# A gate half formed from a copy of the even part in 32 of 288 units of a Fourier and feed-forward kernel

## The chip, the cores and the metric

The kernel runs on one core of a Trainium2 chip. The time is that of one execution on the device, in microseconds (us). The engines are named as in the profile: PE is TensorE (matmuls), PEld its weight loads, DVE is VectorE, ACT is ScalarE, POOL is GpSimd and SP is SyncE, whose queue issues the DMA transfers. PSUM holds the results of matmuls; SBUF holds everything else that is on the core.

## The reference

`x` has shape 8 x 3008 x 256. The reference takes the real part of its two-dimensional Fourier transform (along 3008 and along 256), sees the result as 24064 tokens of 256 values, and sends it through a feed-forward block with a gate:

```python
def _attn_ref(x):
    X = np.fft.fft(x, axis=1)
    X = np.fft.fft(X, axis=2)
    return X.real.astype(np.float32)

def _moe_ref(x, w_gate, w_val, w_out):
    g = x @ w_gate                                   # 256 -> 1536
    gelu = 0.5 * g * (1.0 + erf(g / sqrt(2)))
    val = x @ w_val                                  # 256 -> 1536
    return (gelu * val @ w_out).astype(np.float32)   # 1536 -> 256
```

## The kernel before

**Two rows of tokens from one set of columns.** The transform of a real input is symmetric: row m and row 3008 - m have the same even part and an odd part of opposite sign. For each of the 8 batches the kernel therefore holds only 1505 columns in `Y`, `Y[:, 0]` the even part and `Y[:, 1]` the odd part (channels on the partitions, tokens along the free dimension). The channel transform is folded into the weights once at the start: `WE` multiplies the even part, `WOP` the odd part, each with a gate half (index 0) and a value half (index 1). A token of the plus rows has gate and value WE·even + WOP·odd, one of the minus rows WE·even - WOP·odd. `WOM` is -2 times `WOP`, with one row treated apart (`col_m`): added on to a bank of PSUM that holds the plus rows, it turns them into the minus rows. That one row's share is `nq` (one value a token) times `WN` (one value a channel of the hidden layer), where it has to be added by other engines; `gen_wn` (L411) computes `WN` with 24 one-column matmuls during batch 0.

**Units and pairs.** The first layer is cut into 288 units: 8 batches, in each 3 chunks of columns (`CH`: 481 columns from 1024 on, then 0 to 511, then 512 to 1023), in each chunk 12 blocks of 128 hidden channels. A unit is known by u, its place in its batch by i = u % 36; i below 12 is the chunk of 481 columns. Two units that follow one another, an even and an odd one, are a pair, which shares tiles of two halves: `pv` (PSUM, values), `glp` and `glm` (gelu of the gate for plus and minus rows), `ev` and `dv`.

**The order of the work.** The order on each engine is the order of the program text. In iteration u of the main loop (from L864 on) TensorE gets:

1. `val_even(u)` (L602): one pass of WE into `ps_v`. VectorE makes `ev` = nq·WN + even part of the value.
2. `gate_minus(u-1)` (L613): one pass of WOM on to the bank `ps_g` of unit u-1, which ScalarE has already read once; ScalarE makes `glm`.
3. `val_odd(u-1)` (L634): one pass of WOP on to `ps_v`. If u-1 closes a pair, VectorE makes the plus rows of `h` = glp·pv for both units in one instruction, and `dv` = 2·ev - pv in another, which is the value of the minus rows.
4. `gate_plus(u)` (L618): passes of WE and WOP into a fresh `ps_g`; ScalarE makes `glp`.
5. `minus(u-1)` (L654): if u-1 closes a pair, GpSimd makes the minus rows of `h` = glm·dv for both units.
6. Work for later batches: the fold of x (`fold_x`, L210, on GpSimd: two tensor_tensor and a cast, in some odd units), the first stage of the transform (`a_step`, L462: two matmuls and an evacuation by ScalarE, i from 0 to 11), the second stage (`b_steps`, 47-column matmuls put between the passes, in units from 18 on) with evacuations `Y` by ScalarE.
7. `second(...)` (L877): 8 matmuls of the second layer from a list of steps, `ps_o` <- `Wo_sb`, `h`, evacuated by ScalarE as `osb` and stored by SP's queue. In the later units of a chunk 6 steps are taken where the list is short.

The first chunk of batch 0 goes another way (`kind` 0), without ev and dv.

**What waits for what.** PSUM has two buffers of `ps_g`, so the WE pass of unit u+2's gate needs the readers of unit u's bank to be done; two double buffers of `ps_v` (one a pair); one `ps_o` and one `ps_d`. The folded input `xf` has two buffers, one for even and one for odd batches. `h` has two buffers of 12 x 1024 columns. At u % 12 == 0 the loop makes the second-layer list of the chunk that has just ended; where that is the chunk from column 0 (i = 24) it also copies, on GpSimd, column 960 of the older tile of h into column 1023 of the newer one.

Of the kernel before, what the change touches and what calls it, by code (L numbers as in the profile page):

```python
# [9 lines left out]
FP32 = mybir.dt.float32  # L10
BF16 = mybir.dt.bfloat16
# [16 lines left out]
def _sub(base: bass.AP, free_pattern, free_offset, part_start=0, part_num=None):  # L28
    p_step, p_count = base.ap[0]
    if part_num is None:  # L30
        part_num = p_count - part_start
    pat = [[p_step, part_num]] + [list(x) for x in free_pattern]
    off = base.offset + part_start * p_step + free_offset
    return ap_replace(base, ap=pat, offset=off)
# [3 lines left out]
def kernel(  # L38
# [28 lines left out]
    HJ = 24  # L67
# [24 lines left out]
    WOP = const_pool.tile([128, 2, F], BF16)  # L92
    WOM = const_pool.tile([128, 2, F], BF16)
    Wo_sb = const_pool.tile([128, NFC, C], BF16)
    WNb = const_pool.tile([128, NFC], BF16)
    WN = const_pool.tile([128, NFC], FP32)
    NQs = [const_pool.tile([128, YW], BF16, name=f"nq{i}") for i in range(2)]
    HXF = NFC - NCH * 2
    hx = const_pool.tile([128, HXF, 128], BF16)
    xf_bufs = [const_pool.tile([128, HJ, 2, 128], BF16, name=f"xf{i}") for i in range(2)]  # L100

    Ap = const_pool.tile([128, NG, C], BF16)

# [33 lines left out]
    def glp_tile():  # L137
        return work.tile([128, 2, 512], BF16, tag="glp", bufs=2, name="glp")

    def glm_tile():  # L140
        return work.tile([128, 2, 512], BF16, tag="glm", bufs=3, name="glm")

    def ev_tile():
        return work.tile([128, 2, 512], FP32, tag="ev", bufs=2, name="ev")

    def dv_tile():
        return work.tile([128, 2, 512], FP32, tag="dv", bufs=2, name="dv")

    def osb_tile():
        return work.tile([128, 2, C], FP32, tag="osb", bufs=2, name="osb")  # L150
# [8 lines left out]
    def ps_v():  # L159
        return psum.tile([128, 2, 512], FP32, tag="v", bufs=2, name="ps_v")  # L160
# [48 lines left out]

    def fold_x(b, i, eng, a0=0, an=8, other=None):  # L210
        xt = xins[i]
        xf = xf_bufs[b % 2]
        o0 = (8 * i + a0) * C
        lo = _sub(xt, [[C, an], [1, 127]], a0 * C + 1)
        hi = _sub(xt, [[C, an], [-1, 127]], a0 * C + 255)
        ea = _sub(xf, [[C, an], [1, 127]], o0 + 1)
        od = _sub(xf, [[C, an], [1, 127]], o0 + 129)
        eng.tensor_tensor(ea, lo, hi, op=ALU.add)
        eng.tensor_tensor(od, lo, hi, op=ALU.subtract)
        (other or eng).tensor_copy(  # L220
            _sub(xf, [[C, an], [128, 2]], o0), _sub(xt, [[C, an], [128, 2]], a0 * C))
# [188 lines left out]

    def gen_wn():  # L411
        ps = ps_d()
        for fc in range(NFC):
            for t in range(NCH):
                pe.matmul(
                    ps[:, fc : fc + 1], _sub(wb[(fc // 4 * 512, 1)], [[1, 128]], t * 512 + fc % 4 * 128),
                    CW[:, t, 1, 0:1], start=(t == 0), stop=(t == NCH - 1))
        vec.tensor_copy(WNb[:, :], ps[:, :NFC])
        vec.tensor_copy(WN[:, :], WNb[:, :])

    def gen_tf():
        for i, t in enumerate((TP, TQ, T0P)):
# [38 lines left out]

    def a_step(b, k):  # L462

        xf = xf_bufs[b % 2]
        if "S1" not in st[b]:
            st[b]["S1"] = S1_tile()
        S1 = st[b]["S1"]
        if b == 0:
            ps = (ps_g, ps_vh, ps_o if k % 8 < 4 else ps_d, ps_vh)[k % 4]()
        else:  # L470
            ps = ps_o() if b == 1 and k % 2 and 1 < k < 10 else ps_d()
        for i in range(2):
            jj = 2 * k + i
            on_half(ps, pe.matmul(
                ps[:, i * C : (i + 1) * C], G[:, jj, :], _sub(xf, [[1, C]], jj * C),
                start=True, stop=True))
        dst = _sub(S1, [[1, 2 * C]], 2 * k * C)
        if b == 0 and k % 2 == 0 and k >= 8 or b == 1 and k in (0, 3, 5, 7, 9):
            return on_half(ps, vec.tensor_copy(dst, ps))
        return on_half(ps, act.activation(dst, ps, AF.Copy))  # L480
# [85 lines left out]


    units = []
    for b in range(B):
        for ci in range(len(CH)):  # L570
            for fc in range(NFC):
                units.append((b, ci, fc))
    hs, banks, duos = {}, {}, {}

    def kind(u):
        b, ci, fc = units[u]
# [2 lines left out]
    def open_unit(u):  # L579
        b, ci, fc = units[u]  # L580
        if fc == 0:
            hs[(b, ci)] = h_tile()
        c0, n = CH[ci]
        if u % 2 == 0:
            duos[u // 2] = dict(pv=ps_v(), glp=glp_tile(), glm=glm_tile(), log=[])
            if kind(u):
                duos[u // 2]["ev"] = ev_tile()
        banks[u] = dict(
            d=duos[u // 2], k=u % 2, pv=duos[u // 2]["pv"][:, u % 2, :],
            glp=duos[u // 2]["glp"][:, u % 2, :], glm=duos[u // 2]["glm"][:, u % 2, :],  # L590
            b=b, fc=fc, c0=c0, n=n, nm=n - n % 32, kd=kind(u), fs=slice(fc * 128, (fc + 1) * 128),
            h=hs[(b, ci)], Y=Ys[b], nq=NQs[b % 2], po=0 if n == 512 else 480,
            mo=512 if n == 512 else 0)

    def layer1(r, ps, W, i, eo, n, start):
        m = pe.matmul(
            ps[:, :n], W[:, i, r["fs"]], r["Y"][:, eo, r["c0"] : r["c0"] + n],
            start=start, stop=True, skip_group_check=not start)
        if i:
            apart(r["d"]["log"], r["k"], m)  # L600

    def val_even(u):  # L602
        r = banks[u]
        layer1(r, r["pv"], WE, 1, 0, r["n"], True)
        if r["kd"]:
            nm, fc = r["nm"], r["fc"]
            apart(r["d"]["log"], r["k"], vec.scalar_tensor_tensor(
                r["d"]["ev"][:, r["k"], :nm], r["nq"][:, r["c0"] : r["c0"] + nm],
                WN[:, fc : fc + 1], r["pv"][:, :nm], op0=ALU.mult, op1=ALU.add))
        else:  # L610
            layer1(r, r["pv"], WOP, 1, 1, r["n"], False)

    def gate_minus(u):  # L613
        r = banks[u]
        layer1(r, r["pg"], WOM, 0, 1, r["nm"], False)
        act.activation(r["glm"][:, : r["nm"]], r["pg"][:, : r["nm"]], AF.Gelu)

    def gate_plus(u, fill):  # L618
        r = banks[u]
        n = r["n"]  # L620
        r["pg"] = ps_g()
        layer1(r, r["pg"], WE, 0, 0, n, True)
        fill()
        layer1(r, r["pg"], WOP, 0, 1, n, False)
        fill()
        act.activation(r["glp"][:, :n], r["pg"][:, :n], AF.Gelu)
# [27 lines left out]
    def minus(u):  # L654
        r = banks.pop(u)
        if r["kd"] and r["k"]:
            nm, d = r["nm"], r["d"]
            hm = _sub(r["h"], [[1024, 2], [-1, nm]], (r["fc"] - 1) * 1024 + r["mo"] + nm - 1)
            pool.tensor_tensor(hm, d["glm"][:, :, :nm], d["dv"][:, :, :nm], op=ALU.mult)

# [6 lines left out]
    def windows(b, ci):  # L667
        h = hs[(b, ci)]
        c0, n = CH[ci]
        m0, nb = c0 // 32, n // 32  # L670
        ps = [plus_rows(b, m0 + i) for i in range(nb)]
        ms = [minus_rows(b, m0 + nb - 1 - i) for i in range(nb)]
        blocks = ps + ms if n == 512 else ms + ps
        order = range(8) if n == 512 else (4, 5, 6, 0, 1, 2, 3)
        out = [(h, 128 * w, blocks[4 * w : 4 * w + 4], None) for w in order]
        if c0 == 0:
            out[-1] = out[-1][:3] + (b * T + T // 2,)
        if len(blocks) % 4:
            left = blocks[-2:]
            o = 64 * (b % 2)  # L680
            pool.tensor_copy(hx[:, :, o : o + 64], h[:, :HXF, 896:960])
            pool.tensor_copy(_sub(CW, [[128, NCH * 2], [1, 64]], o), h[:, HXF:, 896:960])
            if b % 2:
                out.append((None, 0, st[b - 1]["left"] + left, None))
            else:
                st[b]["left"] = left
        return out
# [146 lines left out]
    a_first = {4: (0,), 5: (1,), 12: (10,), 13: (11,), 14: (12,), 15: (13,)} | {  # L834
        8 + j: (2 + 2 * j, 3 + 2 * j) for j in range(4)}

    NU = len(units)
    PER = NU // B

    evens = {27 + 2 * q + h: [(0, q, 4 * h, 4 * h + 4)] for q in range(4) for h in range(2)}  # L840
# [8 lines left out]
    for u in range(NU + 2):  # L849
# [22 lines left out]
        def fill(most=2):  # L872
            for _ in range(most):
                if fills:
                    fills.pop(0)()

        def second(n):  # L877
            for _ in range(n):
                if l2q:
                    l2q.pop(0)()  # L880
# [31 lines left out]
            fill()  # L912
        if tail:
            tail()
        if 0 < u <= NU:
            minus(u - 1)
        if u < NU:
            if b + 1 < B and i == (19 if b else 21):
# [26 lines left out]
        if 0 < u <= NU and u % 12 == 0:  # L945
            pb, pi = divmod(u // 12 - 1, 3)
            if CH[pi][0] == 0:
                pool.tensor_copy(hs[(pb, pi)][:, :, 1023:1024], hs[(pb, pi - 1)][:, :, 960:961])
            l2q += l2_steps(pb, pi)
            few = len(l2q) < 96  # L950
        second((6 if few and u % 12 > 5 else 8) if u <= NU else len(l2q))


# [28 lines left out]
```

## Time and profile before

| | |
|---|---|
| runs of the kernel | 631.79, 633.19, 634.82 us; median 633.19 us |
| the profiled execution | 631.74 us, of which the span of the trace 630.0 us |
| granted clock of TensorE | 1.00 |
| busy share of the span | PE 97%, DVE 86%, ACT 75%, POOL 71% |
| WOM passes of the gate | 192 of 512 columns, 96 of 480 columns |
| DMA | 82.39 MB, 131 GB/s over the span |

The busy time is the sum of what the trace records for an engine. Matmuls follow one another in a pipeline, so the duration listed for one (0.38 us for 512 columns) is longer than the time from its start to the next one's. All instructions carry the line of one helper (L25), so groups are told apart by tiles: `ps_g<-Y,WOM` is the pass of WOM for the gate, `h<-glm,dv` GpSimd's minus rows, `h<-glp,ps_v` VectorE's plus rows. In the timelines each row gives the start, the time, the engine, the operation with its tiles, and in brackets the idle time ahead of it with what ended it. A few matmul records are missing from the trace.

### The profile page before, as it was taken

The numbers are of one execution on the slowest core, as the hardware profiler recorded it, in microseconds if no ns is written. First come the engines' busy times: TensorE is split into PE (matmuls) and PEld (weight loads), VectorE is DVE, ScalarE is ACT, GpSimd is POOL, SyncE is SP. The second block draws the span as 40 slices with busy tenths as digits, with TensorE's granted clock in tenths as the row PEclk, the third lists the DMA queues.
The fourth block names the chain that finished last, engine by engine and source line by source line (L and its number), as shares of the span: only waits on it lengthen the run. The fifth ranks groups of instructions, "written<-read, shape, count | busy, mean of one in ns | idle before, by whom it ended". The sixth has DMA issues, their size and how long they took to land.

```text
span 630.0 us, 12878 instructions
## 1 busy us (share of the span) xinstructions
PE 608.2 (97%) x4522; PEld 402.5 (64%) x4580; DVE 541.7 (86%) x654; ACT 471.8 (75%) x956; POOL 448.7 (71%) x472
## 2 busy tenths in 40 slices
PE   3899999999999999999999999999999999999997
PEld 2445666666666666666666666666666666666665
DVE  7698988898988989888888889889888898999891
ACT  8687778877787777877788777877778777766662
POOL 8396987768868788677777697686885564555452
PEclk9999999999999999999999999999999999999999
DMA  8997423562236512673245532375223611212113
GB/s 313 360 265 247 138 64 114 171 193 90 75 114 207 196 43 75 186 231 102 51 129 177 182 95 76 101 217 192 56 64 97 188 47 44 62 48 52 45 40 84
DMA packets 65458, 82.39 MB, mean 131 GB/s; under 512 B 8298, under 2 KB 58986, under 8 KB 62578
## 3 DMA queue, kind: packets, MB, share of 16 engines
q1 hardware_dynamic: 63682, 80.65, 41.5%
q0 software_dynamic: 1552, 0.79, 0.9%
q8 instruction: 36, 0.59, 0.4%
q14 instruction: 28, 0.23, 0.1%
q10 hardware_dynamic: 160, 0.13, 0.1%
HBM read 45.08 MB, written 37.25 MB: 131 GB/s over the span
## 4 chain that ended last, share of the span: by engine, by line
PE 83%; DVE 9%; POOL 3%; ACT 2%; issue 1%; DMA 1%; SPq 0%; DVEq 0%; ACTq 0%; POOLq 0%
PE ps_o L25 35%; PE ps_g L25 25%; PE ps_v L25 18%; PE ps_d L25 6%; DVE h L25 4%; DVE dv L25 3%; POOL h L25 2%; DVE ev L25 1%; DMA gate<-z 1%; ACT glp L25 1%; DVE S L25 0%; ACT glm L25 0%; ACT S L25 0%; ACT WE L25 0%; DMA out_dram<-osb 0%
## 5 line engine op out<-in xcount | busy, mean ns | idle before, releaser
L25 POOL TENSOR_TENSOR h<-glm,dv 128x1024 bf16<-128x1024 bf16 (+1 forms) x138 | 290.9, 2108 | 157.1 <-DVE dv L25 113.1
L25 PE MATMUL ps_o<-Wo_sb,h 128*128 128x256 bf16 x2136 | 277.7, 272 | 0.4 <-ACT osb L25 0.2
L25 ACT ACTIVATE glm<-ps_g 128x512 bf16<-128x512 f32 (+1 forms) x288 | 169.4, 588 | 111.8 <-PE ps_g L25 75.2
L25 DVE SCALAR_TENSOR_TENSOR ev<-nq,WN,ps_v 128x512 f32<-128x512 bf16 (+1 forms) x276 | 201.9, 734 | 59.0 <-PE ps_v L25 43.4
L25 PEld LDWEIGHTS <-h 128*128 128x128 bf16 x2208 | 210.9, 97 | 54.5 <-issue 0.9
L25 DVE TENSOR_TENSOR h<-glp,ps_v 128x1024 bf16<-128x1024 bf16 (+2 forms) x150 | 173.0, 1153 | 11.1 <-POOL h L25 5.2
L25 ACT ACTIVATE glp<-ps_g 128x512 bf16<-128x512 f32 (+1 forms) x288 | 169.9, 590 | 10.9 <-PE ps_g L25 1.9
L25 DVE SCALAR_TENSOR_TENSOR dv<-ev,ps_v 128x1024 f32<-128x1024 f32 (+1 forms) x138 | 164.8, 1194 | 0.0
L25 POOL TENSOR_TENSOR xf<-xin 128x254 bf16<-128x254 f32 x168 | 118.1, 724 | 0.3 <-DMA xin<-in_x_dram 0.3
L25 PE MATMUL ps_g<-Y,WOM 128*128 128x512 bf16 (+1 forms) x288 | 107.7, 374 | 0.3
L25 PE MATMUL ps_v<-Y,WOP 128*128 128x512 bf16 (+1 forms) x288 | 107.7, 374 | 0.1
L25 PE MATMUL ps_v<-Y,WE 128*128 128x512 bf16 (+1 forms) x282 | 105.7, 375 | 0.9 <-DVE dv L25 0.5
L25 PE MATMUL ps_g<-Y,WOP 128*128 128x512 bf16 (+1 forms) x278 | 103.9, 374 | 1.7
L25 PE MATMUL ps_g<-Y,WE 128*128 128x512 bf16 (+1 forms) x249 | 92.9, 373 | 0.0
L25 PEld LDWEIGHTS <-WOP 128*128 128x128 bf16 x576 | 55.8, 97 | 52.8 <-ACT WOP L25 0.4
L25 PEld LDWEIGHTS <-WE 128*128 128x128 bf16 x576 | 55.9, 97 | 31.5 <-issue 0.9
L25 ACT ACTIVATE osb<-ps_o 128x512 f32<-128x512 f32 x93 | 54.8, 589 | 17.6 <-PE ps_o L25 13.6
L25 PEld LDWEIGHTS <-Ap 128*128 128x128 bf16 (+1 forms) x561 | 40.8, 95 | 35.2 <-issue 1.7
L25 ACT ACTIVATE S<-ps_d 128x512 bf16<-128x512 f32 x80 | 47.4, 593 | 0.1
L25 PEld LDWEIGHTS <-G 128*128 128x128 bf16 x213 | 21.0, 100 | 32.9 <-ACT G L25 8.6
L25 ACT ACTIVATE Y<-ps_d 128x192 bf16<-128x192 f32 (+4 forms) x142 | 34.0, 340 | 0.5 <-PE ps_d L25 0.5
L25 PEld LDWEIGHTS <-WOM 128*128 128x128 bf16 x300 | 29.2, 97 | 5.5 <-issue 0.7
(139 smaller groups left out, 260.8 us busy)
## 6 DMA issues: line engine op xcount, KB each, us to landing
out_dram<-osb SPq DMA_DIRECT2D x358, 64.0 KB
xin<-in_x_dram SPq DMA_DIRECT2D x16, 1024.0 KB
Ap<-z SPq DMA_DIRECT2D x24, 512.0 KB
xin<-in_x_dram SPq DMA_DIRECT2D x8, 896.0 KB
z<-S SPq DMA_DIRECT2D x7, 768.0 KB
z<-S SPq DMA_DIRECT2D x8, 512.0 KB
nq<-nrow SPq DMA_DIRECT2D x8, 376.2 KB
z<-S SPq DMA_DIRECT2D x11, 256.0 KB
```

Source lines behind the costliest of these rows:

```text
L25: return lambda *a, **k: self._tc.keep_in_program_order(call(*a, **k))
```

## The change

In 32 units, each the first of its pair, the gate takes two passes in place of three (`two`). They are i = 24 in batch 0, i = 0, 4, 8, 16 and 26 in batches 1 to 6, and i = 14 in batch 7.

In such a unit u, `gate_plus` does the WE pass alone, and ScalarE copies the bank, which then holds the even part, into `ge[:, 0]` (SBUF, f32). The WOP pass is done in iteration u+1, in the place of the WOM pass, and gives the plus rows; ScalarE makes `glp` from it. VectorE makes `ge[:, 0]` = 2·`ge[:, 0]` - bank, GpSimd adds `ge[:, 1]`, which it formed as nq·(2·WN) when unit u was opened. In iteration u+2 the call of `minus(u+1)` stands at the end, behind `second`: there ScalarE takes the gelu of `ge[:, 0]` into `glm[:, 0]`, and GpSimd makes the minus rows of h as before.

Three things go with it. `WNb` and `WN` get a gate half, so `gen_wn` computes 24 columns, with 48 matmuls. `xf` has one buffer. Column 960 of h is saved in `WNb[:, 0]` when the first chunk's list is made (a GpSimd copy more), and column 1023 is copied from there at i = 24.

```diff
-    WNb = const_pool.tile([128, NFC], BF16)
-    WN = const_pool.tile([128, NFC], FP32)
+    WNb = const_pool.tile([128, 2, NFC], BF16)
+    WN = const_pool.tile([128, 2, NFC], FP32)
...
-    xf_bufs = [const_pool.tile([128, HJ, 2, 128], BF16, name=f"xf{i}") for i in range(2)]
+    xf = const_pool.tile([128, HJ, 2, 128], BF16)
...
+    def ge_tile():
+        return work.tile([128, 2, 512], FP32, tag="ge", bufs=2, name="ge")
...
     def gen_wn():
         ps = ps_d()
-        for fc in range(NFC):
+        for k in range(2 * NFC):
+            i, fc = divmod(k, NFC)
             for t in range(NCH):
                 pe.matmul(
-                    ps[:, fc : fc + 1], _sub(wb[(fc // 4 * 512, 1)], [[1, 128]], t * 512 + fc % 4 * 128),
+                    ps[:, k : k + 1], _sub(wb[(fc // 4 * 512, i)], [[1, 128]], t * 512 + fc % 4 * 128),
                     CW[:, t, 1, 0:1], start=(t == 0), stop=(t == NCH - 1))
-        vec.tensor_copy(WNb[:, :], ps[:, :NFC])
-        vec.tensor_copy(WN[:, :], WNb[:, :])
+        f = lambda t: _sub(t, [[1, 2 * NFC]], 0)
+        vec.tensor_copy(f(WNb), ps[:, : 2 * NFC])
+        vec.tensor_scalar(f(WN), f(WNb), 2.0, None, op0=ALU.mult)
+        vec.tensor_copy(WN[:, 1, :], WNb[:, 1, :])
...
+    def apart_gate(u):
+        b, ci, fc = units[u]
+        i = u % (NU // B)
+        return i in ((24,) if b == 0 else (14,) if b == B - 1 else (0, 4, 8, 16, 26))
...
+            if apart_gate(u):
+                ge, nm = ge_tile(), n - n % 32
+                duos[u // 2]["ge"] = ge
+                pool.tensor_scalar(
+                    ge[:, 1, :nm], NQs[b % 2][:, c0 : c0 + nm], WN[:, 0, fc : fc + 1], None,
+                    op0=ALU.mult)
...
     def gate_minus(u):
         r = banks[u]
+        n, nm = r["n"], r["nm"]
+        if r["two"]:
+            layer1(r, r["pg"], WOP, 0, 1, n, False)
+            act.activation(r["glp"][:, :n], r["pg"][:, :n], AF.Gelu)
+            ge = r["d"]["ge"]
+            vec.scalar_tensor_tensor(
+                ge[:, 0, :nm], ge[:, 0, :nm], 2.0, r["pg"][:, :nm], op0=ALU.mult, op1=ALU.subtract)
+            pool.tensor_tensor(ge[:, 0, :nm], ge[:, 0, :nm], ge[:, 1, :nm], op=ALU.add)
+            return
...
         layer1(r, r["pg"], WE, 0, 0, n, True)
         fill()
+        if r["two"]:
+            act.activation(r["d"]["ge"][:, 0, : r["nm"]], r["pg"][:, : r["nm"]], AF.Copy)
+            return
...
     def minus(u):
...
             nm, d = r["nm"], r["d"]
+            if d["two"]:
+                act.activation(d["glm"][:, 0, :nm], d["ge"][:, 0, :nm], AF.Gelu)
...
+            pool.tensor_copy(WNb[:, 0, :], h[:, :, 960:961])
...
-        if 0 < u <= NU:
+        late = 0 < u <= NU and u % 2 == 0 and banks[u - 1]["d"]["two"]
+        if 0 < u <= NU and not late:
             minus(u - 1)
...
-                pool.tensor_copy(hs[(pb, pi)][:, :, 1023:1024], hs[(pb, pi - 1)][:, :, 960:961])
+                pool.tensor_copy(hs[(pb, pi)][:, :, 1023:1024], WNb[:, 0, :])
...
         second((6 if few and u % 12 > 5 else 8) if u <= NU else len(l2q))
+        if late:
+            minus(u - 1)
```

More of the change, by code (lines that the diff above doesn't have):

```diff
@@ L211, in fold_x @@
         xt = xins[i]
-        xf = xf_bufs[b % 2]
         o0 = (8 * i + a0) * C
@@ L462, in a_step @@
     def a_step(b, k):
-        xf = xf_bufs[b % 2]
         if "S1" not in st[b]:
@@ L568 @@
     units = []
+    NU = B * len(CH) * NFC
     for b in range(B):
@@ L584, in open_unit @@
         if u % 2 == 0:
-            duos[u // 2] = dict(pv=ps_v(), glp=glp_tile(), glm=glm_tile(), log=[])
+            duos[u // 2] = dict(two=apart_gate(u), pv=ps_v(), glp=glp_tile(), glm=glm_tile(), log=[])
             if kind(u):
                 duos[u // 2]["ev"] = ev_tile()
+            if apart_gate(u):
[4 more added lines that the diff above has]
+                    op0=ALU.mult)
         banks[u] = dict(
@@ L591, in open_unit @@
             b=b, fc=fc, c0=c0, n=n, nm=n - n % 32, kd=kind(u), fs=slice(fc * 128, (fc + 1) * 128),
-            h=hs[(b, ci)], Y=Ys[b], nq=NQs[b % 2], po=0 if n == 512 else 480,
+            two=apart_gate(u), h=hs[(b, ci)], Y=Ys[b], nq=NQs[b % 2], po=0 if n == 512 else 480,
             mo=512 if n == 512 else 0)
@@ L608, in val_even @@
                 r["d"]["ev"][:, r["k"], :nm], r["nq"][:, r["c0"] : r["c0"] + nm],
-                WN[:, fc : fc + 1], r["pv"][:, :nm], op0=ALU.mult, op1=ALU.add))
+                WN[:, 1, fc : fc + 1], r["pv"][:, :nm], op0=ALU.mult, op1=ALU.add))
         else:
@@ L835 @@
         8 + j: (2 + 2 * j, 3 + 2 * j) for j in range(4)}
-    NU = len(units)
     PER = NU // B
```

## The prediction

> **What bounds the kernel now.** I read the table of busy time first, then the shares of the chain that ended last.
>
> ```profile
> PE 608.2 (97%) x4522; PEld 402.5 (64%) x4580; DVE 541.7 (86%) x654; ACT 471.8 (75%) x956; POOL 448.7 (71%) x472
> ...
> PE 83%; DVE 9%; POOL 3%; ACT 2%; issue 1%; DMA 1%; SPq 0%; DVEq 0%; ACTq 0%; POOLq 0%
> ```
>
> TensorE is busy for 97% of the span and holds the chain, so a pass less is worth its whole length as long as the matmuls behind it have their inputs. VectorE at 86% is next. Since an average hides stages, I read the timelines of TensorE, VectorE and GpSimd around the five places where the change works in batch 3, first for a 512-column unit, i=16 (it opens at 280.89):
>
> ```profile
> 282.85 0.38 PE L25 MATMUL ps_v<-Y,WE 128*128 128x512 bf16 x1
> 283.06 0.38 PE L25 MATMUL ps_g<-Y,WOM 128*128 128x512 bf16 x1
> 283.28 0.38 PE L25 MATMUL ps_v<-Y,WOP 128*128 128x512 bf16 x1
> ...
> 285.45 0.38 PE L25 MATMUL ps_g<-Y,WE 128*128 128x512 bf16 x1
> ```
>
> Starts, not durations, give the price: 283.06 to 283.28, so 0.2155 us a pass (0.203 in the 480-column units, read in the same way), against 0.38 listed.
>
> ```profile
> 281.98 1.22 DVE L25 TENSOR_TENSOR h<-glp,ps_v 128x1024 bf16<-128x1024 bf16 x1
> 283.11 1.21 DVE L25 SCALAR_TENSOR_TENSOR dv<-ev,ps_v 128x1024 f32<-128x1024 f32 x1
> 284.24 0.74 DVE L25 SCALAR_TENSOR_TENSOR ev<-nq,WN,ps_v 128x512 f32<-128x512 bf16 x1
> 285.22 0.75 DVE L25 SCALAR_TENSOR_TENSOR ev<-nq,WN,ps_v 128x512 f32<-128x512 bf16 x1 [0.24 <-PE ps_v L25]
> ```
>
> VectorE runs these one behind the other. In 512-column pairs of units it needs 1.13+1.13+0.66+0.66 = 3.58 us, start to start, of TensorE's 3.90 (two units of 1.95): 0.32 us free in a pair. In the 480-column chunk it is some 3.4 of 4.21.
>
> **What the change removes.** 32 WOM passes of the gate: 18 of 480 columns by 0.203 and 14 of 512 by 0.2155, 6.67 us. Then a wait:
>
> ```profile
> DVE h L25 <- POOL h L25: 5.2, 7, 0.8
> ```
>
> At i=24 a GpSimd copy reads an old h tile whose buffer VectorE's next h is to write, so that h waits. In batch 3 TensorE gets a gap of 0.22 us ahead of unit 28 and 0.12 behind it (starts 305.97 and 306.62, due 0.22 and 0.34 earlier); batch 7 shows 0.87. The new copy takes its column from WNb, saved long before: 6 x 0.34 + 0.87 = 2.9 us. The copies into WNb are 12 elements each (0.24 us for such a copy), on a GpSimd that is idle beside them; without that cover 0.24 us of lateness for the next h.
>
> **What it adds.** gen_wn doubles: its 24 one-column matmuls took 0.74 us (42.37 on, with the 512-column one behind it due), so 24 more are +0.72 on TensorE. Three VectorE instructions there lengthen by 12 elements: nothing. One buffer for xf: each fold comes after the a_step that reads the same slice, by several units; no wait. SP's queue is not changed.
>
> In each two-pass unit u, ScalarE's gelu of glm becomes a copy of the even part (same shape; 0.60 us), earlier by one unit, in an ACT gap (0.71 and 0.77 us idle in front of glm at 281.53 and 283.54). WOP comes into the place of WOM in unit u+1. Then:
> - VectorE: one more ge <- ge,ps_g, 512 wide, f32. Between half of dv's 1.21 us for 1024 and ev's 0.75; I take ev (0.66 to the next start), which is nearest in shape.
> - GpSimd: a tensor_scalar into ge and an f32 add, neither in the trace. The first lies between the 512-element copy's 0.603 and 0.79: a tensor_scalar of 129 f32 elements took 0.380, 1.3 times what copies of 256 and 512 (0.394, 0.603) give at 129. I take 0.60, the nearest in size; at 0.79 the add at i=8 and i=26 comes 0.19 later, 1.9 us over 10 places. For the add, the h rows (1024: 2.145; 960: 2.023) give 1.906 ns an element and 0.19 fixed, so 1.17 for 512 and 1.10 for 480; by the small f32 row NA<-Ap,TB (64 elements, 0.349) at most 1.46. I take 1.17, since the 254-element folds from f32 lie on that line.
> - ScalarE: the gelu of ge is put at the end of unit u+2, behind the add.
>
> ge also waits for the glp gelu, which reads the same bank and is done before VectorE comes to it, and WOP for the copy, done 0.1 us or more before. Neither binds. Two other waits do. WE of unit u+2 takes the PSUM buffer that ge reads, so it waits for VectorE. And the late gelu waits for the GpSimd add; behind it on ScalarE stands glm(u+2), behind that glp(u+3), and WOM(u+3) on TensorE waits for glp(u+3).
>
> **One place worked out (i=16).** Unit 18's WE was due at 285.45 - 0.2155 = 285.23. VectorE comes to ge behind ev(17), at 284.24 + 0.66 = 284.90, and ends it at 285.64; 0.06 us to TensorE: stall 0.47. That alone is twice what the pass saved. The add waits behind h (284.46 + 2.15) and ends at 287.77; the late gelu is due about 287.25 and takes 0.5, so glm(18) starts at 288.33 instead of 287.8. WOM(19) then waits 0.1 us, and 0.5 in even batches, whose units 18 to 23 have six second-layer steps, not eight. Net +0.34, or +0.74.
>
> **i=26.** VectorE's wait is gone, so h starts at 302.70, dv 303.83, ev 304.96, ge 305.62, ending 306.36; WE(28) is due 306.29: 0.13. GpSimd:
>
> ```profile
> 303.29 0.24 POOL L25 COPY h<-h 128x12 bf16<-128x12 bf16 x1
> 303.45 1.41 POOL L25 TENSOR_TENSOR xf<-xin 128x254 bf16<-128x254 f32 x2
> 304.80 0.20 POOL L25 CAST xf<-xin 128x4 bf16<-128x4 f32 x1
> 306.08 2.15 POOL L25 TENSOR_TENSOR h<-glm,dv 128x1024 bf16<-128x1024 bf16 x1 [1.09 <-DVE dv L25]
> ```
>
> After the cast (305.0) tensor_scalar to 305.65, h to 307.8, add to 308.93. ScalarE:
>
> ```profile
> 307.96 0.67 ACT L25 ACTIVATE Y<-ps_d 128x161 bf16<-128x161 f32 x4
> 308.83 0.60 ACT L25 ACTIVATE glm<-ps_g 128x512 bf16<-128x512 f32 x1 [0.20 <-PE ps_g L25]
> 309.47 0.60 ACT L25 ACTIVATE glp<-ps_g 128x512 bf16<-128x512 f32 x1
> ```
>
> Everything here is 0.42 earlier, so the late gelu is due at 308.2, waits until 308.99, and glm(28) starts at 309.49, glp(29) at 310.0. WOM(29) was at 310.47, due 310.05, and goes at 310.66: 0.61. Net -0.22 + 0.13 + 0.61 = +0.52, or +0.17 with the 0.34 of the vanished wait.
>
> **The 480-column places.** i=0: fold ends 251.02, tensor_scalar 251.62, h 253.72, add 254.9; gelu due 254.68; WOM(3) 0.30 late, WE(2) 0.05: net +0.15. i=4: the add ends 262.74, the gelu is blocked 0.3, WOM(7) is due 264.70 and glp(7) done before: net -0.20. i=8: from h at 259.64 GpSimd has 1.99 + 1.10 + 1.56 + 1.99 + 1.56 + 0.60 + 1.99 + 1.11 (h, add, fold, h, fold, tensor_scalar, h, add) to 271.54; the gelu is due 270.83; 0.36 on TensorE by WOM(11) and a late osb: net +0.16.
>
> **Sum.** Batches 1, 3, 5: 0.15 - 0.20 + 0.16 + 0.34 + 0.17 = 0.62 each, 1.86; batches 2 and 4: 1.02, 2.04; batch 6, with no folds, +0.12; batch 0 (i=24) +0.10; batch 7 (i=14) +0.60 - 0.87 = -0.27; gen_wn +0.72. Together +4.6 us. The profiled execution (631.74; span 630.0) becomes 636.3; it stands at the low end of the runs, so on their median, 633.19, I forecast **637.8**.
>
> The half of it that decides is ScalarE's queue: whether glm waits behind a blocked gelu. The nearest row is VectorE's: with 0.77 us of wait in front of h at 303.56, dv and ev behind it went late too. For ScalarE, the trace of before holds no instruction that a blocked one clearly held up. The Trainium skill, TensorE: Matmul & The Clock Gate, section "Architectural detail: the array is 16× 32×32, not 1× 128×128", says that ScalarE's and VectorE's queues are strictly first in, first out; by it the sum stands at +4.6, and were ScalarE able to pass, it would be -4.2 (third rival).
>
> **Rivals.**
> - *Late gelu half hidden* (633.4). The blocks behind ScalarE add up to 0.30 x 5 + 0.36 x 5 + 0.1 x 3 + 0.5 x 3 + 0.61 x 5 + 0.35 x 2 = 8.8 us of the sum; a gelu due 0.3 us later everywhere than I read would halve them. For: the due times are read off ScalarE starts with evacuations between. Against: i=8 and i=26 are 0.7 to 0.8 over.
> - *Late gelu wholly hidden, faster* (629.0): 4.6 - 8.8 = -4.2; only VectorE's 0.47 at i=16 and the small ones are left. It decides where the add ends before ScalarE has done the last osb or Y of unit u+2, that is GpSimd 0.8 us quicker than my chain at i=26. For: GpSimd is only 71% busy. Against: its h can't start before dv ends.
> - *Everything hidden* (624.3): -6.67 - 2.9 + 0.72 = -8.9. Needs VectorE 0.47 us early at i=16, against the rows above.
> - *VectorE becomes the bound* (645): with ge a 512 pair needs 3.58 + 0.66 = 4.24 of 3.90; if late ev and dv hold ps_v up two pairs later (0.34 us at each of the 14 places, 4.8) and the add costs 1.46 (0.29 at the 10 places that are late, 2.9), 4.6 + 7.7 = +12.3. Against: dv(8) would end at 288.6, and val_even(20) is due at 289.2.
>
> That the passes don't leave TensorE can't be: the program has 32 fewer.
>
> **Chances.** Forecast 0.47 (its own range 635.5 to 640.5), half hidden 0.19, wholly hidden 0.24, everything 0.03, VectorE bound 0.07. A difference of 0.5% (3.2 us: under 630.0, over 636.4) is about what a measurement here tells from none. Faster: 0.20 of the 0.24, the 0.03, 0.02 of half hidden: 0.25. Slower: 0.37 + 0.07 + 0.01 = 0.45. Same 0.30. Range 628.2 to 642: below lies a part of the hidden cases (some 0.09), above the VectorE bound and a little of the forecast (0.1).
>
> **What would show it.** At i=16 a wait of PE ps_g on DVE ge near 0.5 us; ACT glm waits on POOL ge of 0.3 to 0.8 at i=0, 8, 26, with WOM of the next unit but one starting late; no DVE h wait on POOL h. If ACT never waits for POOL longer than 0.1 us, the forecast is wrong and 629 right; if ev or dv hold up ps_v, it is 645.

## The result and the profile after

| | before | changed |
|---|---|---|
| median of the runs | 634.01 us (631.79 to 635.02, 4 runs) | 652.88 us (651.91 to 653.42, 4 runs) |
| profiled execution | 631.74 us, span 630.0 | 653.38 us, span 651.6 |

The changed kernel is slower: ratio 1.0301, 95% interval 1.0267 to 1.0334. The forecast was 637.8 and the range ended at 642. Parts 1 and 4 of the page of the changed kernel (busy time; shares of the chain that ended last):

```profile
PE 606.4 (93%) x4514; PEld 400.2 (61%) x4572; DVE 561.8 (86%) x687; ACT 480.7 (74%) x988; POOL 534.8 (82%) x544
...
PE 58%; DVE 14%; POOL 12%; ACT 7%; issue 4%; DMA 2%; SPq 1%; ACTq 0%; POOLq 0%; DVEq 0%
```

TensorE's share fell from 97% to 93% in a longer span: it has less work and waits more. Its share of the chain went from 83% to 58%, GpSimd's from 3% to 12%. GpSimd's busy time rose by 86 us, from 448.7; the forecast had counted 32 x (0.60 + 1.17), some 57. The waits of the changed kernel (us in total, times, longest):

```profile
ACT glm L25 <- POOL ge L25: 36.7, 38, 1.8
...
PE ps_g L25 <- ACT glp L25: 20.9, 22, 1.5
...
PE ps_g L25 <- DVE ge L25: 1.5, 7, 0.2
```

The first two are the two ends of one chain, and neither was there before: ScalarE waits for GpSimd's `ge`, and TensorE for a glp gelu that stands behind. The third is WE(18) at i=16; its listed 0.2 us is less than the 0.38 us that it costs in the table below, because the listed 0.38 us of the matmul ahead of it runs some 0.16 us into the gap. The wait of VectorE's h on GpSimd's h (5.2 us before) is gone, as the change meant it. The groups of GpSimd's and VectorE's new instructions, with the mean in ns behind the comma:

```profile
L25 POOL TENSOR_SCALAR ge<-nq,WN 128x480 f32<-128x480 bf16 x18 | 26.8, 1487 | 0.0
L25 POOL TENSOR_SCALAR ge<-nq,WN 128x512 f32<-128x512 bf16 x14 | 21.9, 1567 | 0.0
L25 POOL TENSOR_TENSOR ge<-ge 128x480 f32<-128x480 f32 x18 | 21.7, 1206 | 0.0
L25 POOL TENSOR_TENSOR ge<-ge 128x512 f32<-128x512 f32 x14 | 17.8, 1272 | 0.0
...
L25 DVE SCALAR_TENSOR_TENSOR ge<-ge,ps_g 128x512 f32<-128x512 f32 x14 | 9.5, 681 | 0.0
```

The add and VectorE's part are near what was worked out (1.10 and 1.17; 0.75). The tensor_scalar takes 1.49 and 1.57 us, not 0.60, and lies above the bound of 0.79 that was set for it. What that does is seen at i=26 of batch 3 in the timelines of GpSimd, ScalarE and TensorE:

```profile
317.43 1.57 POOL L25 TENSOR_SCALAR ge<-nq,WN 128x512 f32<-128x512 bf16 x1
318.97 2.15 POOL L25 TENSOR_TENSOR h<-glm,dv 128x1024 bf16<-128x1024 bf16 x1
321.08 1.27 POOL L25 TENSOR_TENSOR ge<-ge 128x512 f32<-128x512 f32 x1
```

```profile
319.95 0.67 ACT L25 ACTIVATE Y<-ps_d 128x161 bf16<-128x161 f32 x4
322.38 0.63 ACT L25 ACTIVATE glm<-ge 128x512 bf16<-128x512 f32 x1 [1.77 <-POOL ge L25]
322.92 0.58 ACT L25 ACTIVATE glm<-ps_g 128x512 bf16<-128x512 f32 x1
323.40 0.59 ACT L25 ACTIVATE glp<-ps_g 128x512 bf16<-128x512 f32 x1
```

```profile
322.18 0.38 PE L25 MATMUL ps_v<-Y,WE 128*128 128x512 bf16 x1
322.40 0.21 PE L25 MATMUL ps_d<-TP,Ap 128*128 128x47 bf16 x2
324.04 0.38 PE L25 MATMUL ps_g<-Y,WOM 128*128 128x512 bf16 x1 [1.43 <-ACT glp L25]
```

Read from the end: WOM of unit 29 goes at 324.04 because glp(29) ran at 323.40; that stood behind glm(28), whose matmul had gone at 320.34; that stood behind the gelu of ge, idle for 1.77 us; that waited for the add, the add for h, and h for the tensor_scalar. VectorE had ended dv of that pair at 317.51 (316.30 + 1.21), so h could have begun at 317.65 (the trace of before shows 0.14 us from dv's end to h), had GpSimd been free.

All 288 WOP passes of the values are in both traces, so the distance from each to the next, less the same distance before, shows where time went. By place, in us each time it occurs (the saved pass and what follows it; the copy gain of 0.34 at i=26 is in it; batch 6 is one sum over its five places, and the last row is the total):

| place | predicted | changed | of it stalls |
|---|---|---|---|
| i=0 | +0.15 | +0.91 | 1.11 at WOM(3) |
| i=4 | -0.20 | -0.20 | none |
| i=8 | +0.16 | +0.91 | 0.98 + 0.13 |
| i=16, odd / even batch | +0.34 / +0.74 | +0.36 / +0.79 | 0.38 at WE(18), 0.20 / 0.63 behind |
| i=26 | +0.17 | +1.10 | 0.07 + 1.59 |
| batch 6 | +0.12 | +1.18 | 1.11 at i=0, none at i=8, 0.38 + 0.63 at i=16, 0.07 + 0.37 at i=26 |
| batch 0, i=24 | +0.10 | +1.37 | 1.59 |
| batch 7, i=14 | -0.27 | +0.28 | 0.38 + 0.99 |
| gen_wn | +0.72 | +2.05 | 0.60 for the matmuls, 1.92 after them, 0.47 made up |
| all | +4.6 | +21.1 | |

The spans differ by 21.6 us (0.46 of it ahead of the first unit); the medians differ by 18.9. The trace of before is of an execution at the fast end of its runs (631.74) and that of the changed kernel of one at the slow end (653.38), which is why the spans differ by more than the medians.

### The profile page after: what moved, and what is told of

Its sections match the earlier page's. It is cut to its first block, busy times and chain, and to the rows that moved or that the text cites. A ratio compares the mean times of both kernels' runs of the same rounds, so it can differ in the third digit from the quotient of the medians.

```text
span 651.6 us, 12999 instructions
## 1 busy us (share of the span) xinstructions
PE 606.4 (93%) x4514; PEld 400.2 (61%) x4572; DVE 561.8 (86%) x687; ACT 480.7 (74%) x988; POOL 534.8 (82%) x544
## 4 chain that ended last, share of the span: by engine, by line
PE 58%; DVE 14%; POOL 12%; ACT 7%; issue 4%; DMA 2%; SPq 1%; ACTq 0%; POOLq 0%; DVEq 0%
PE ps_o L25 24%; PE ps_g L25 18%; PE ps_v L25 12%; POOL h L25 7%; DVE h L25 5%; DVE dv L25 4%; POOL ge L25 4%; PE ps_d L25 4%; ACT glm L25 4%; DVE ev L25 2%; ACT glp L25 2%; DVE ge L25 1%; DMA Ap<-z 1%; POOL xf L25 1%; DMA gate<-z 1%
## 5 line engine op out<-in xcount | busy, mean ns | idle before, releaser
L25 ACT ACTIVATE glm<-ps_g 128x512 bf16<-128x512 f32 (+1 forms) x256 | 150.4, 588 | 82.3 <-PE ps_g L25 55.0
L25 PE MATMUL ps_g<-Y,WOM 128*128 128x512 bf16 (+1 forms) x256 | 95.8, 374 | 21.3 <-ACT glp L25 20.9
L25 POOL TENSOR_SCALAR ge<-nq,WN 128x480 f32<-128x480 bf16 (+1 forms) x32 | 48.7, 1522 | 0.0
L25 ACT ACTIVATE glm<-ge 128x480 bf16<-128x480 f32 (+1 forms) x32 | 19.7, 615 | 33.7 <-POOL ge L25 33.7
L25 PEld LDWEIGHTS <-G 128*128 128x128 bf16 x213 | 21.1, 101 | 34.8 <-ACT G L25 8.6
```

The source lines that it names most:

```text
L25: return lambda *a, **k: self._tc.keep_in_program_order(call(*a, **k))
```

## The experiments

The theory to test, called Q in what follows, is the chain above: the late gelu stands in ScalarE's queue until GpSimd's add is done, and GpSimd's queue is late by the tensor_scalar. Its rivals: VectorE's added instruction or the order itself costs the time (V); any GpSimd instruction from bf16 to f32 is dear (F); GpSimd has too much work altogether (B). "Before" is the kernel before, on the same chip.

### Without GpSimd's two instructions

The share nq·(2·WN) of the gate's minus rows is left out in the 32 units:

```diff
-                pool.tensor_scalar(ge[:, 1, :nm], NQs[b % 2][:, c0 : c0 + nm], WN[:, 0, fc : fc + 1], ...)
...
-            pool.tensor_tensor(ge[:, 0, :nm], ge[:, 0, :nm], ge[:, 1, :nm], op=ALU.add)
```

> The changed kernel without GpSimd's tensor_scalar and add on ge (the nq share of the gate's minus rows is left out in the 32 units). Theory Q (the late gelu waits in ScalarE's queue for GpSimd, whose queue the 1.5 us tensor_scalar has made late): the gelu then needs VectorE alone, the stalls of 1.1 us at i=0 and i=8, 1.6 at i=26 and 0.2 to 0.6 behind i=16 go, some 24 us together, and only about 0.4 of wait on ge at i=16 is left: 628 to 630 us. Rival V (VectorE's extra instruction, or the order with minus at the end of the unit, is what costs): those stalls stay, above 645.

Measured: 628.01 us (10 runs), before 632.39; ratio 0.9931, interval 0.9910 to 0.9952. Every stall behind the late gelu is gone: i=0, 4 and 8 each -0.20, i=26 -0.49, and no wait of ScalarE for `ge` is left. What is left at i=16 is the 0.38 at WE(18), and 0.09 in even batches. So VectorE's part (V) costs 0.38 there and 0.07 at i=26, and the stalls behind the late gelu hang on GpSimd's two instructions. The doubled gen_wn is still in this version, with 1.4 us in its trace.

### A copy in the place of the tensor_scalar

The factor 2·WN is left out in the 32 units:

```diff
-                pool.tensor_scalar(ge[:, 1, :nm], NQs[b % 2][:, c0 : c0 + nm], WN[:, 0, fc : fc + 1], ...)
+                pool.tensor_copy(ge[:, 1, :nm], NQs[b % 2][:, c0 : c0 + nm])
```

> The changed kernel with GpSimd's tensor_scalar (1.49 and 1.57 us) replaced by a plain copy of nq into the same f32 tile (the factor WN is left out in the 32 units). Theory Q: the copy takes 0.6 to 0.7, every add comes 0.9 earlier, the stalls at i=0, 8 and 26 shrink by that to about what was predicted (0.3, 0.3, 0.65): 637 to 640 us. Rival F (any GpSimd instruction that turns bf16 into f32 costs 1.5 us): no change, 652 to 654. Rival V: no change either, but with a copy of 0.6.

Measured: 637.06 us (4 runs), before 632.39; ratio 1.0064, interval 1.0044 to 1.0084. The copy takes 0.587 and 0.611 us, also from bf16 to f32, so F falls. The medians differ by 4.7 us (by the interval 2.8 to 5.3); the forecast for a step of 0.60 was +4.6. By place (predicted in brackets): i=0 -0.04 (+0.15), i=4 -0.20 (-0.20), i=8 -0.07 (+0.16), i=16 +0.37 and +0.79 (+0.34 and +0.74), i=26 +0.09 (+0.17), batch 6 +0.11 (+0.12). The stalls at i=0, 8 and 26 come out a little smaller than predicted, and gen_wn larger (+1.7 instead of +0.72). Between the first and the last unit the trace is 3.6 us longer than before, so the places bear the forecast out, but the agreement of 4.7 with 4.6 is in part luck: two errors of opposite sign, and noise of the medians.

### The late gelu one unit later

```diff
+    due_minus = None
...
-        if late:
-            minus(u - 1)
+        if due_minus is not None:
+            minus(due_minus)
+        due_minus = u - 1 if late else None
```

> The changed kernel with the late gelu of ge and GpSimd's h put one unit later, at the end of unit u+3; everything is computed. Theory Q: the add has long ended when ScalarE comes to the gelu, no glm stands behind a blocked one, and the 1.1 to 1.6 us stalls at WOM(u+3) go: 629 to 632 us. Rival B (GpSimd has too much work, so h comes late wherever the gelu stands): the wait moves to dv or to the second layer, 640 or more.

Measured: 630.51 us (8 runs), before 632.39; ratio 0.9964, interval 0.9942 to 0.9985. With the same work on every engine, 1.57 us of tensor_scalar included, another place in the queues moves the time from 652.9 to 630.5. The call moves two instructions, the late gelu on ScalarE and the minus rows of h on GpSimd; this run doesn't tell them apart, but the add that the gelu waits for stands where it stood. GpSimd, then ScalarE, in this version's timelines at i=26 of batch 3:

```profile
307.64 1.57 POOL L25 TENSOR_SCALAR ge<-nq,WN 128x512 f32<-128x512 bf16 x1
309.18 2.15 POOL L25 TENSOR_TENSOR h<-glm,dv 128x1024 bf16<-128x1024 bf16 x1
311.29 1.28 POOL L25 TENSOR_TENSOR ge<-ge 128x512 f32<-128x512 f32 x1
```

```profile
311.04 0.60 ACT L25 ACTIVATE glm<-ps_g 128x512 bf16<-128x512 f32 x1
311.67 0.60 ACT L25 ACTIVATE glp<-ps_g 128x512 bf16<-128x512 f32 x1
312.60 0.60 ACT L25 ACTIVATE osb<-ps_o 128x512 f32<-128x512 f32 x1 [0.33 <-PE ps_o L25]
313.09 0.62 ACT L25 ACTIVATE glm<-ge 128x512 bf16<-128x512 f32 x1
```

The add ends at 312.57 as late as ever, but glm(28) and glp(29) are past by then, at 311.04 and 311.67, and the gelu of ge comes at 313.09 with no wait in front of it. i=26 is -0.43 here and was +1.10. B falls: h of that pair is later still, and no engine's wait for GpSimd's h is in this trace.

### gen_wn doubled, alone

The new `gen_wn` of the change in the kernel before, the gate half not used:

```diff
-        for fc in range(NFC):
+        for k in range(2 * NFC):
+            i, fc = divmod(k, NFC)
...
-        vec.tensor_copy(WNb[:, :], ps[:, :NFC])
-        vec.tensor_copy(WN[:, :], WNb[:, :])
+        vec.tensor_copy(f(WNb), ps[:, : 2 * NFC])
+        vec.tensor_scalar(f(WN), f(WNb), 2.0, None, op0=ALU.mult)
+        vec.tensor_copy(WN[:, 1, :], WNb[:, 1, :])
```

> The kernel before with gen_wn alone doubled (24 more one-column matmuls and the three VectorE instructions on WNb and WN; the gate half is not used). If the small VectorE instructions from SBUF to SBUF (1.27 and 1.45 us for 24 and 12 elements in the changed kernel) hold the pairs behind them up as there: +2.0 us, 636. By the price predicted for it, matmuls alone: +0.7 us, 634.7.

Measured: 635.48 us (10 runs), before 632.39; ratio 1.0032, interval 1.0015 to 1.0050. That is 2.0 us by the ratio, 3.1 by the medians; its trace shows 3.5 in batch 0. By each of them it is more than the matmuls alone (0.60), but the price of the chain of VectorE instructions isn't settled by this run; the next one takes it apart.

### WN from PSUM

To the version with the gelu one unit later:

```diff
-        vec.tensor_scalar(f(WN), f(WNb), 2.0, None, op0=ALU.mult)
-        vec.tensor_copy(WN[:, 1, :], WNb[:, 1, :])
+        vec.tensor_scalar(f(WN), ps[:, : 2 * NFC], 2.0, None, op0=ALU.mult)
+        vec.tensor_copy(WN[:, 1, :], ps[:, NFC : 2 * NFC])
```

> The version with the late gelu at the end of unit u+3, with one thing changed: WN is formed from PSUM and not from the bf16 copy in SBUF. Theory P (a VectorE instruction that both reads and writes SBUF alone waits here until GpSimd's fold is done): the two instructions take under 0.3 us in place of 1.3 to 1.5, and the stall of TensorE behind gen_wn, 2.2 us in batch 0, goes to 0.7 or less: 1.5 to 2 us less than that version, 628.5 to 629. Rival (the chain of small instructions costs by itself): no change, 630 to 631.

Measured: 628.10 us (6 runs), before 633.85; ratio 0.9917, interval 0.9903 to 0.9932. The three VectorE instructions in the timeline of the changed kernel, and two of GpSimd's folds beside them:

```profile
44.77 0.17 DVE L25 CAST WNb<-ps_d 128x24 bf16<-128x24 f32 x1
44.98 1.27 DVE L25 TENSOR_SCALAR WN<-WNb 128x24 f32<-128x24 bf16 x1
46.28 1.45 DVE L25 CAST WN<-WNb 128x12 f32<-128x12 bf16 x1
```

```profile
44.80 1.41 POOL L25 TENSOR_TENSOR xf<-xin 128x254 bf16<-128x254 f32 x2
46.16 0.20 POOL L25 CAST xf<-xin 128x4 bf16<-128x4 f32 x1
46.30 1.40 POOL L25 TENSOR_TENSOR xf<-xin 128x254 bf16<-128x254 f32 x2
```

The one from PSUM takes 0.17 us. The two from SBUF to SBUF take some eight times as long for 24 and 12 elements, and each ends when GpSimd's pair of folds does: 46.25 beside 46.21, 47.73 beside 47.70. The run of gen_wn alone shows the same (47.68 beside 47.64, 49.17 beside 49.14). In the new version:

```profile
44.55 0.17 DVE L25 CAST WNb<-ps_d 128x24 bf16<-128x24 f32 x1
44.63 0.17 DVE L25 TENSOR_SCALAR WN<-ps_d 128x24 f32<-128x24 f32 x1
44.84 0.17 DVE L25 COPY WN<-ps_d 128x12 f32<-128x12 f32 x1
```

All three take 0.17 with the folds running on, and the stall behind gen_wn (2.16 in the version it was made from) is gone; between the first and the last unit the trace is 1.9 us shorter. The Trainium skill, SBUF — State Buffer, section "Who interferes with whom", says that VectorE and GpSimd share one pair of SBUF ports, held for a whole instruction, and that VectorE's copies, casts and tensor_scalars can take it; the trace agrees, with two such instructions at 1.27 and 1.45 us that end with GpSimd's and take 0.17 when they read PSUM. No run here has them between SBUF tiles with GpSimd idle.

### The saved column alone

```diff
+    h960 = const_pool.tile([128, NFC], BF16)
...
+            pool.tensor_copy(h960[:, :], h[:, :, 960:961])
...
-                pool.tensor_copy(hs[(pb, pi)][:, :, 1023:1024], hs[(pb, pi - 1)][:, :, 960:961])
+                pool.tensor_copy(hs[(pb, pi)][:, :, 1023:1024], h960[:, :])
```

> The kernel before with only the saved column: column 960 of h is copied into a small tile when the first chunk's list is made, and column 1023 is taken from there. If the wait of VectorE on GpSimd at i=24 is worth what the gaps on TensorE showed (6 x 0.34 + 0.87): 2.9 us less than before, 629 to 630. If the wait is filled by another one behind it: no difference.

Measured: 630.84 us (6 runs), before 633.85; ratio 0.9955, interval 0.9938 to 0.9972. The distances show -0.34 at i=26 in batches 1 to 6 and -0.87 in batch 7, to the hundredth what was read off the gaps.

### Which places pay

In the version with WN from PSUM:

```diff
-        return i in ((24,) if b == 0 else (14,) if b == B - 1 else (0, 4, 8, 16, 26))
+        return i in ((24,) if b == 0 else (0, 4, 8, 26))
```

> The version of the run before this one with the two-pass units at i=0, 4, 8 and 26 in batches 1 to 7 and i=24 in batch 0, so without i=16 and i=14. The table of unit lengths gives i=16 as -0.22 and +0.38 (+0.09 in even batches): without it 0.16 to 0.25 less in each of six batches, and batch 7 gains at four places instead of losing 0.33 at one: 626.5 to 628 us. If i=16 pays for itself elsewhere, no difference to the run before.

Measured: 628.42 us (6 runs), before 633.85; ratio 0.9914, interval 0.9896 to 0.9933: not told apart from the version it was made from. Batches 1 to 5 gain what the table gave (-0.88 each against -0.58 to -0.70), but batch 7 loses: +0.23 against -0.52. Its pairs of units stall by 0.30 to 0.38 at i=1, 5, 9 and 27. The trace shows the wait of i=16 there, WE(u+2) on VectorE's `ge`: for the first of them, `ge` starts at 545.44 right behind `ev`, ends at 546.09, and WE(2) goes at 546.14. A pair of 480-column units takes TensorE 3.78 us in batch 7 (2 x 1.89 in the trace of before), not 4.21, and VectorE needs 3.4 and 0.57 for `ge`, so VectorE is the bound there. That no other cause adds to it was not tested. So:

```diff
-        return i in ((24,) if b == 0 else (0, 4, 8, 26))
+        return i in ((24,) if b == 0 else () if b == B - 1 else (0, 4, 8, 26))
```

> The version with the late gelu at the end of unit u+3, WN from PSUM and two-pass units at i=0, 4, 8 and 26, now without any in batch 7 (i=24 in batch 0 and those of batches 1 to 6 stay). In the run with four of them in batch 7 the pairs of units there lost 0.3 each, 1.1 us in that batch against the kernel with the saved column alone: so 1.1 us less, 0.99 of the kernel before, 626.5 to 628. If batch 7 isn't the reason, no difference.

Measured: 626.78 us (6 runs), before 633.79; ratio 0.9896, interval 0.9875 to 0.9917. This is 1.0% below before, the lowest ratio of all versions. Its interval overlaps those of the two versions ahead of it; the traces tell them apart, with -5.8 us against before between the first and the last unit, where those two have -4.2 and -4.8.

### What the tensor_scalar costs

Split into a copy to f32 and a product in place, in the changed kernel:

```diff
+                pool.tensor_copy(ge[:, 1, :nm], NQs[b % 2][:, c0 : c0 + nm])
                 pool.tensor_scalar(
-                    ge[:, 1, :nm], NQs[b % 2][:, c0 : c0 + nm], WN[:, 0, fc : fc + 1], None,
+                    ge[:, 1, :nm], ge[:, 1, :nm], WN[:, 0, fc : fc + 1], None,
                     op0=ALU.mult)
```

> The changed kernel with GpSimd's tensor_scalar split: a copy of nq into f32, then the product with WN in place, f32 to f32. If the 1.5 us come with reading bf16 in that instruction, the second takes about 0.6 to 0.7 as the earlier f32 rows say (127 to 129 elements in 0.38), together 1.3, and the time is a little below the changed kernel's, about 649. If a product with a value for each partition costs 2.5 ns an element whatever the input, together 2.1, and the time is 660 or more.

Measured: 675.99 us (one run). The copy takes 0.586 and 0.610, the product from f32 still 1.485 and 1.566: the input's type is not the reason. And 0.6 us more on GpSimd in each of the 32 units cost 23 us more in all. The stalls grow by 0.64 at i=0, 0.79 at i=8, 0.43 at i=16 and some 0.66 at i=26, and in three batches another 1.3 to 1.4 us came one unit behind i=26; at i=4 there is still none. So where the late gelu already holds up TensorE, a further delay on GpSimd comes through nearly in full or more.

The same instruction where VectorE is idle:

```diff
+        if u == NU:
+            t = ev_tile()
+            nq, wn = NQs[1][:, 512:1024], WN[:, 0:1]
+            for dst, src in ((t[:, 0, :], nq), (t[:, 0, :], t[:, 0, :]), (t[:, 0, :128], t[:, 0, :128])):
+                for _ in range(2):
+                    pool.tensor_scalar(dst, src, wn, None, op0=ALU.mult)
+            pool.tensor_copy(t[:, 1, :], nq)
+            for _ in range(2):
+                pool.tensor_tensor(t[:, 0, :], t[:, 0, :], t[:, 1, :], op=ALU.add)
```

> The kernel before with nine GpSimd instructions on an unused tile behind its last h, where VectorE is idle: two tensor_scalar by WN from bf16 to f32 and two from f32 to f32, 512 wide, two of 128, a copy of 512, two f32 additions of 512. If 1.57 us is the instruction's own price, the first four take 1.5 to 1.6 here too. If it is made by VectorE working beside it in all 32 places, they take 0.6 to 0.95 here, as the early rows of 127 and 129 elements had said. The additions 1.17 to 1.27. The time: within 0.5% of before.

Measured: 634.62 us (one run), before 633.79. Its groups of shapes:

```profile
L25 POOL TENSOR_SCALAR ev<-nq,WN 128x512 f32<-128x512 bf16 x2 | 3.1, 1571 | 0.1
L25 POOL TENSOR_SCALAR ev<-ev,WN 128x512 f32<-128x512 f32 x2 | 3.1, 1564 | 0.2
...
L25 POOL TENSOR_SCALAR ev<-ev,WN 128x128 f32<-128x128 f32 x2 | 1.2, 604 | 0.2
```

1.57 us is the instruction's own price, with no VectorE beside it. From 128 to 512 elements it grows by (1564 - 604) / 384 = 2.5 ns an element. The two additions take 1.26 us each, near the 1.27 of the changed kernel.

The same product by a two-input instruction, in the changed kernel:

```diff
-                pool.tensor_scalar(ge[:, 1, :nm], NQs[b % 2][:, c0 : c0 + nm], WN[:, 0, fc : fc + 1], ...)
+                pool.tensor_tensor(
+                    ge[:, 1, :nm], NQs[b % 2][:, c0 : c0 + nm], _sub(WN, [[0, nm]], fc), op=ALU.mult)
```

> The changed kernel with GpSimd's tensor_scalar replaced by a tensor_tensor of nq with WN repeated along the free dimension: the same product. By the line of the two-input rows (0.19 + 1.906 ns an element) 1.10 and 1.17 us in place of 1.49 and 1.57; each late gelu comes 0.3 to 0.4 earlier and the time is some 6 us below the changed kernel's, 646 to 648. If the repeated operand or the product costs what the tensor_scalar costs: 652 to 654.

Measured: 644.73 us (one run), a little below what was expected, because the instruction takes 0.988 and 1.042 us, less than the line of the two-input rows gives. The product is cheaper with two inputs than as a tensor_scalar, and the time follows its duration: 637.1 us at 0.59 to 0.61, 644.7 at 0.99 to 1.04, 652.9 at 1.49 to 1.57.

## Why the prediction was wrong

The direction and the mechanism were right: the saved passes are given back where glm waits in ScalarE's queue behind a gelu that waits for GpSimd. The step that failed is the price of GpSimd's tensor_scalar, "between the 512-element copy's 0.603 and 0.79 ... I take 0.60, the nearest in size". It measured 1.49 and 1.57. With an instruction of the assumed price in its place the kernel stood 4.7 us above before, where 4.6 was forecast (3.6 by the places in its trace).

The bound was wrong in its kind. The upper end came from an early tensor_scalar of 129 elements (0.380), another form with two operations; the form used here takes 0.604 for 128. So the form alone makes a factor of 1.6, and why two operations are the cheaper form no run shows. One short row can't separate a fixed cost from a cost for each element either. It was then scaled by a ratio, and the cost of being wrong was put at 1.9 us for 0.19 at ten places. That is 10 us for each us of delay; measured it was (652.9 - 637.1) / 0.93, some 17, since i=0 and the places in batches 0 and 7 pay for it too, and not i=8 and i=26 alone. Such a term needed a wider bound.

- **Removed passes**: right (0.20 and 0.22 at each place).
- **The copy wait, 2.9 us**: right, shown alone at 3.0 (633.85 - 630.84).
- **WE(18) behind ge at i=16**: predicted 0.47, measured 0.38, since ge takes 0.68 and not 0.75. WE(28) 0.13, measured 0.07.
- **ScalarE's queue**: right in place and cause. The late gelu waits 1.05, 1.55 and 1.77 us at i=0, 8 and 26, where 0.3 to 0.8 was named. At i=26 TensorE loses 1.59 instead of 0.61: about the tensor_scalar's 0.97 more and 0.1 of the add. In batch 3 glm(28), whose matmul had gone at 320.34, ran at 322.92, behind the blocked gelu: ScalarE did not pass it.
- **gen_wn, "three VectorE instructions there lengthen by 12 elements: nothing"**: wrong by 1.3 us. The trace of before held the hint: WN <- WNb, 12 elements in 0.61 us, next to 0.16 for the same size from PSUM, ended at 45.12 where GpSimd's pair of folds, begun at 43.70, ended at 45.10:

```profile
44.32 0.16 DVE L25 CAST WNb<-ps_d 128x12 bf16<-128x12 f32 x1
44.51 0.61 DVE L25 CAST WN<-WNb 128x12 f32<-128x12 bf16 x1
```

- **One buffer for xf: no wait**: right; all idle time ahead of the 168 folds was 0.3 us before and 0.5 us after.
- **Rivals**: the late gelu wholly hidden (629.0; the prediction calls its -4.2 the third rival, and it is the second of its list) did not happen to this kernel, but is close to what the version with the gelu one unit later measured (630.5). Half hidden (633.4) did not happen either: with an instruction of the assumed price the stalls behind ScalarE add up to 8.2 us, of 8.8 predicted. "VectorE becomes the bound" did not happen here: no pass of TensorE waited for ev or dv. With two-pass units in batch 7 it did, by way of `ge`.

## What to carry to other kernels

A pass taken off the busiest engine was worth its length here only where the replacement's last instruction was ready by the place it has in its queue; where a queue is in order, ask what stands behind the instruction that waits, and first try to put it later. Price an operation that the trace doesn't show by a range that its rows can't contradict, and where the sum changes by ten times the error, measure it. Small VectorE instructions between SBUF tiles were not small here while GpSimd worked (0.61 to 1.45 us for 12 elements); from PSUM they were (0.16 to 0.17).

## What the runs showed of the hardware

- GpSimd's tensor_scalar by a value for each partition costs 1.57 us for 128 x 512, from bf16 or f32, with VectorE busy or idle; a tensor_tensor with that value repeated 1.04, a copy 0.61.
- A 12-element VectorE cast from SBUF to SBUF took 1.45 us beside GpSimd's folds; a copy of as many elements from PSUM took 0.17 beside them.
- A late ScalarE instruction on GpSimd's result cost TensorE nothing at i=4, where it waited 0.18 us, and 1.59 us at i=26, where it waited 1.77; one unit later it cost at most 0.07 at either.
